# Reordering the start of an attention + expert-layer kernel: two bias-row loads, and two pairs of casts

## The chip, the core and the metric

The kernel runs on one core of a Trainium2 chip. The metric is the device time of one execution in microseconds (us). A core has five engines that each work through their own instructions in order: TensorE (PE in the profile), VectorE (DVE), ScalarE (ACT), GpSimd (POOL) and Sync (SP), which here only issues transfers. Sixteen transfer (DMA) engines move the data; transfers are issued from the queues of SP, ACT and POOL.

## The reference

Inputs are q, k, v of shape (8, 8, 576, 64), gates s of shape (8, 8, 576), w_in (512, 2048) and w_out (2048, 512), all float32. The output is (4608, 512) float32.

```python
scores = scale * np.matmul(q, k.transpose(0, 1, 3, 2))       # scale = 1/8
s_pos = np.maximum(s, 0.0)
cum = np.cumsum(s_pos, axis=-1)
bias = -(cum[:, :, :, None] - cum[:, :, None, :])
scores = np.where(causal, -1000000000.0, scores + np.minimum(bias, 0.0))
attn = softmax(scores)
x = np.matmul(attn, v)            # heads put side by side: (4608, 512)
h = x @ w_in
g = h * np.clip(h + 3.0, 0.0, 6.0) / 6.0
out = g @ w_out
```

Each of the 64 heads is one causal attention whose scores get a bias, the running sum of the gates at the key less that at the query. Then every token goes through a two-layer network with the hard-swish in between.

## The kernel before

Two heads make a pair; there are 32 pairs (NP), four to a batch. The main loop (L576) goes over the pairs. In pass p TensorE computes the transposed scores of pair p in blocks (`scores`, `corner`), the output of the attention (`av`), and the transposes of the next pair (`transpose`, L217, for pairs 0 to 8; later pairs go through a transposing DMA). From pass 4 on, groups of the first and second layer (`m1`, `m2`) stand between them. The order on every engine is the order in which the code is written: nothing is reordered by a scheduler.

What a pair needs before its scores can start:

- q and k in float32 (`load_qk`, L110, two transfers of 288 KB), in one of three buffers `raws`;
- their cast to float16 into `tok` (`cast_qk`, L188, two instructions; `tok` has two buffers);
- the transposes of `tok` on TensorE (L221, six for q and six for k) and four copies from PSUM into `qks` (L230; q's two on VectorE, k's on ScalarE or shared), one of three slots;
- the bias rows: four rows per head (partitions 64 to 67) that add the bias inside the same matmul, copied by DMA from `aug`, where they lie for all 64 heads (`load_aug`, L138, two transfers of 9 KB, one a head). The slot's lower half must have been filled by `set_stair` (L508) before.

It needs v later (`load_v`, L126 twice with 128 KB and L130 with 32 KB, in rows of 256 bytes; cast by GpSimd, `cast_v`, L200 and L201).

`aug` itself is computed at the start: VectorE takes the running sum (L545), ScalarE writes its negative as one row (L548, "the bias copy"), VectorE writes three more (L549 to L553). The first bias rows can leave only after that.

The start of the program, in the order of Sync's queue: the gates, q of pair 0, v of pair 0, q and k of pair 1; then bias rows of pair 0, which wait for `aug`; then q and k of pair 2, v of pair 1, q and k of pair 3, v of pair 2; then, from pass 0, the bias rows of pair 2, q and k of pair 4, v of pair 3; from pass 1 the bias rows of pair 3, q and k of pair 5, v of pair 4; and so on. ScalarE's queue brings k of pair 0 and constants. GpSimd issues the bias rows of pair 1, and later the weights: `next_weights` (L585) in passes 0 and 2 to 6, 1 MB for each half of w_in and 512 KB for each quarter of w_out, cast to float16 on the way. Pairs from 6 on have their bias rows issued by GpSimd as well.

Pairs are counted from 0 in this text; "pairs two and three" in the change's name are pairs 1 and 2 here.

The casts of pair 0 are on ScalarE (L559), after the bias copy. Those of all later pairs are on GpSimd; pair 1's stand behind the bias rows that GpSimd issues and behind v of pair 0. In pass p GpSimd casts q and k of pair p + 2, then v of pair p + 1 (not in pass 0), then issues weights.

Before the first data arrive, TensorE runs 44 matmuls on constants (L537).

Of the kernel before, what the change touches and what calls it, by code (L numbers as in the profile page):

```python
# [18 lines left out]
def kernel(  # L19
# [10 lines left out]
    nc = tc.nc  # L30
# [8 lines left out]
    PPB = H // 2  # L39
# [60 lines left out]
    def raw6(p):  # L100
        return raws[p % NRAW][0:96].rearrange("p (i h e d) -> p i h e d", i=2, h=2, e=6)

    def raw9(p):
        return raws[p % NRAW][:, 0 : 18 * D].rearrange("p (i t d) -> p i t d", i=2, t=9)

    def load_qk(p, i, eng):
        b, h0 = p // PPB, 2 * (p % PPB)
        src = (q, k)[i][b, h0 : h0 + 2]
        if p < NPE:
            eng.dma_start(  # L110
                out=raw6(p)[:, i].rearrange("p h e d -> p h (e d)"),
                in_=src.rearrange("h (p e) d -> p h (e d)", e=6),
            )
        else:
            eng.dma_start(
                out=raw9(p)[:, i],
                in_=src.rearrange("h s d -> (h s) d").rearrange(
                    "(t p) d -> p t d", p=128
                ),
            )  # L120

    def load_v(p, eng):
        b, h0 = p // PPB, 2 * (p % PPB)
        vraw = vraws[p % NRAW]
        for hh in range(2):
            eng.dma_start(  # L126
                out=vraw[:, hh, 0:4, :],
                in_=v[b, h0 + hh, 0:512, :].rearrange("(t p) d -> p t d", p=128),
            )
        eng.dma_start(  # L130
            out=vraw[0:64, :, 4, :],
            in_=v[b, h0 : h0 + 2, 512:SEQ, :].rearrange("h p d -> p h d"),
        )

    def load_aug(p, eng):
        for hh in range(2):
            g = 2 * p + hh
            eng.dma_start(  # L138
                out=qks[p % NQK][64:68, hh, :, 64 * hh : 64 * hh + SEQ],
                in_=aug[g : g + 1, :, :, :],  # L140
            )
# [21 lines left out]
    def next_weights(n):  # L163
        for _ in range(n):
            if w_chunks:
                fn, c = w_chunks.pop(0)
                fn(c)
# [15 lines left out]
    def cast_qk(p, eng_q, eng_k):  # L183
        tok = work.tile([128, 24 * D], F16, tag="tok", name="tok")
        if p < NPE:
            tok = tok[0:96].rearrange("p (i e h d) -> p i e h d", i=2, e=6, h=2)
            for i, eng in enumerate((eng_q, eng_k)):
                eng(out=tok[:, i].rearrange("p t h d -> p h t d"), in_=raw6(p)[:, i])  # L188
        else:
            tok = tok[:, 0 : 18 * D]  # L190
            for i, eng in enumerate((eng_q, eng_k)):
                eng(  # L192
                    out=tok[:, 9 * D * i : 9 * D * (i + 1)],
                    in_=raws[p % NRAW][:, 9 * D * i : 9 * D * (i + 1)],
                )
        toks[p] = tok

    def cast_v(p):
        vraw, va = vraws[p % NRAW], vas[p % NQK]
        nc.gpsimd.tensor_copy(out=va[:, :, 0:4, 0:64], in_=vraw[:, :, 0:4, :])  # L200
        nc.gpsimd.tensor_copy(out=va[0:64, :, 4, 0:64], in_=vraw[0:64, :, 4, :])  # L201
# [15 lines left out]
    def transpose(p, i):  # L217
        tok, qk = toks[p], qks[p % NQK]
        pt = t_bank(i == 1, "pt")
        for e in range(6):  # L220
            nc.tensor.transpose(  # L221
                pt[:, 96 * e : 96 * (e + 1)],
                tok[:, i, e].rearrange("p h d -> p (h d)"),
                ident[0:96, 0:96],
            )
        for hh in range(2):
            r = 64 * hh
            on_act = i == 1 and (hh == 0 or p % 2 == 0)
            copy = nc.scalar.copy if on_act else nc.vector.tensor_copy
            copy(  # L230
                out=qk[0:64, hh, i, r : r + SEQ].rearrange("p (t e) -> p t e", e=6),
                in_=pt[r : r + 64, 0:SEQ].rearrange("p (e t) -> p t e", e=6),
            )
# [7 lines left out]
    def crossbar_qk(p):  # L241
        J[p] = work.tile([128, 9, 128], F16, tag="jt", name="jt")
        nc.sync.dma_start_transpose(out=J[p], in_=toks[p])
# [129 lines left out]
    def norm(p, hh):  # L373
        o = O.pop((p, hh))
        if hh == 0:
            X[p] = work.tile([128, 5, 2, D], F16, tag="x", name="x")
        rl = work.tile([128, 5, 1], F32, tag="rl", name="rl")
        nc.vector.reciprocal(out=rl, in_=o[:, :, 64:65])
        nc.vector.tensor_tensor(  # L379
            out=X[p][:, :, hh, :],  # L380
            in0=o[:, :, 0:64],
            in1=rl.to_broadcast([128, 5, 64]),
            op=ALU.mult,
        )
# [121 lines left out]
    def set_stair(i, copy):  # L506
        for hh in range(2):
            copy(  # L508
                out=qks[i][64:128, hh, :, 64 * hh : 64 * hh + 640].rearrange(
                    "p i (t c) -> p i t c", c=128  # L510
                ),
                in_=stair_sb[64:128, :, None, :].to_broadcast([64, 2, 5, 128]),
            )
# [21 lines left out]
    for i in range(44):  # L535
# [9 lines left out]
    nc.vector.tensor_tensor_scan(  # L545
        out=c8, data0=ones, data1=spos, initial=0.0, op0=ALU.mult, op1=ALU.add
    )
    nc.scalar.mul(out=aug[:, 0, 0, :], in_=c8, mul=-1.0)  # L548
    nc.vector.tensor_copy(out=aug[:, 1, 1, :], in_=c8)  # L549
    r1 = work.tile([NHEADS, SEQ], F32, tag="s_all", bufs=1, name="r1")  # L550
# [5 lines left out]

    nc.vector.tensor_scalar_add(out=neg_sb, in0=masks[:, 0:128], scalar1=-65504.0)

    cast_qk(0, nc.scalar.copy, nc.scalar.copy)  # L559
    transpose(0, 0)  # L560
    load_aug(0, nc.sync)
    for p in (2, 3):
        for i in range(2):
            load_qk(p, i, nc.sync)
        if p == 2:
            load_v(1, nc.sync)
    load_v(2, nc.sync)
    transpose(0, 1)
    set_stair(2, nc.vector.tensor_copy)
    load_aug(1, nc.gpsimd)  # L570
    cast_v(0)
    cast_qk(1, nc.gpsimd.tensor_copy, nc.gpsimd.tensor_copy)
    cast_v(1)


    for p in range(NP):  # L576
        nxt = p + 1 < NP
        if p + 2 < NP:
            load_aug(p + 2, nc.sync if p < PPB else nc.gpsimd)
            cast_qk(p + 2, nc.gpsimd.tensor_copy, nc.gpsimd.tensor_copy)  # L580
            if p + 2 >= NPE:
                crossbar_qk(p + 2)
        if p and nxt:
            cast_v(p + 1)
        next_weights({0: 1, 2: 1, 3: 1, 4: 1, 5: 1, 6: 1}.get(p, 0))  # L585
        if p + 3 < NP:
            for m in (p + 3, p + 4):
                late = NPE <= m < NPE + 2
                if 3 < m < NP and late == (m == p + 3):
                    for i in range(2):  # L590
                        load_qk(m, i, nc.sync)
            load_v(p + 3, nc.sync)

        def get(i):
            if p + 1 < NPE:
                transpose(p + 1, i)
            elif nxt:
                spread(p + 1, i)

        if p < PPB:  # L600
            scores(p, 0, 0)
            scores(p, 0, 1)
            get(0)
            scores(p, 0, 2)
            corner(p)
            if p:
                av(p - 1, 1, 0)
                av(p - 1, 1, 1)
                norm(p - 1, 1)
            scores(p, 1, 0)  # L610
            get(1)
            scores(p, 1, 1)
            av(p, 0, 0)
            scores(p, 1, 2)
            if p:
                transpose_x(p - 1)
            av(p, 0, 1)
            norm(p, 0)
            continue

        if p == PPB:
            av(p - 1, 1, 0)
            av(p - 1, 1, 1)
            norm(p - 1, 1)
            scores(p, 0, 0)
            scores(p, 0, 1)
            transpose_x(p - 1)
            early[0] = False
            scores(p, 0, 2)
            get(0)  # L630
            group()
            group()
        else:
            scores(p, 0, 0)
            get(0)
            group()
            scores(p, 0, 1)
            av(p - 1, 1, 0)
            group()
            scores(p, 0, 2)  # L640
            av(p - 1, 1, 1)
            norm(p - 1, 1)
            group()
        corner(p)
        group()
        if p > NPE:
            x_done[0] = p - 1
        scores(p, 1, 0)
        get(1)
        group()  # L650
        scores(p, 1, 1)
        av(p, 0, 0)
        if p >= NPE:
            crossbar_x(p - 1)
        group()
        scores(p, 1, 2)
        if PPB < p < NPE:
            transpose_x(p - 1)
        group()
        av(p, 0, 1)  # L660
        norm(p, 0)
        group()

    p = NP - 1
# [38 lines left out]
```

## Time and profile before

Four runs took 368.99, 369.27, 369.56 and 373.45 us, a median of 369.41. The profiled execution is the one of 373.45 us; its span from the first to the last instruction is 371.6 us.

| | us busy | share of the span |
|---|---|---|
| TensorE, matmuls | 350.5 | 94% |
| VectorE | 241.3 | 65% |
| ScalarE | 223.0 | 60% |
| GpSimd | 105.8 | 28% |

The 16 transfer engines are 80 to 90% busy or more in nearly all of the first three quarters of the span, and at 10% or so in most of the last quarter. Sync's queue moves 48.26 of the 54.02 MB, GpSimd's 4.70 MB.

The page says of the chain of work that ended last: 86% of the span is TensorE's, 4% transfers, 4% VectorE's. It lists the longest idle time of TensorE ahead of the score matmuls (L292): 7.3 us that ended with the landing of bias rows, in three waits of 1.1, 3.65 and 2.5 us.

How to read what follows. Times are from the start of the span. A line of a timeline gives start, length (of all its instructions together), engine and source line, operation, output <- inputs, count, and in brackets the idle time before it and what ended it. SPq and POOLq are instruction queues that issue transfers; the time of such a line is that of issuing, not of moving the data. A line of the table by stages gives the stretch, its length, then for PE, PEld (weight loads), DVE, ACT and POOL the busy time with the number of instructions, then the granted TensorE clock, the busy share of the transfer engines and GB/s. Buffer numbers are left out of names: `qk<-aug` is any pair's bias rows, `raw` q and k in float32, `vraw` v in float32, `tok` q and k in float16.

### The profile page before, as it was taken

Reading aid. Unit: us, or ns where it says so; the run is one execution under the profiler, and the core shown is the slowest. Engines: PE = TensorE matmul, PEld = TensorE weight load, DVE = VectorE, ACT = ScalarE, POOL = GpSimd, SP = SyncE. Lnnn points to the kernel's source line nnn. Section 1 sums busy time; section 2 is a strip of 40 time slices with the busy share of each in tenths; the row PEclk is TensorE's granted clock in tenths of the full one; section 3 lists DMA queues with packets and bytes.
Section 4 is the critical chain, followed back from the end, with each engine's and each line's share of the span. In section 5 each row is a group of like instructions: output and inputs, shape, how many; then the busy total and the mean of one; then the engine's idle time right before and its main releaser. Section 6 shows DMA issues by size and latency. Waiting matters only on the chain.

```text
span 371.6 us, 7713 instructions
## 1 busy us (share of the span) xinstructions
PE 350.5 (94%) x2897; PEld 204.5 (55%) x2897; DVE 241.3 (65%) x539; ACT 223.0 (60%) x388; POOL 105.8 (28%) x201
## 2 busy tenths in 40 slices
PE   6786698979999999999999999999999999999996
PEld 6565465635555555555555555555555544444442
DVE  7474769777777877777777777777775554454531
ACT  6675687846667766666666666666666334334310
POOL 3746183443334333333333333333300000000000
PEclk9998989989999999999999999999999999999999
DMA  8999999998999999999987999998311011010012
GB/s 200 201 209 182 245 220 216 155 206 169 178 172 183 196 215 178 141 215 180 177 180 147 207 178 151 203 180 149 83 49 48 28 49 38 28 56 31 28 56 86
DMA packets 147774, 54.02 MB, mean 145 GB/s; under 512 B 137520, under 2 KB 141312, under 8 KB 147736
## 3 DMA queue, kind: packets, MB, share of 16 engines
q1 hardware_dynamic: 143736, 48.26, 66.4%
q0 software_dynamic: 3360, 4.70, 7.0%
q10 hardware_dynamic: 640, 0.56, 0.6%
q8 instruction: 23, 0.38, 0.5%
q14 instruction: 15, 0.12, 0.1%
HBM read 37.11 MB, written 9.44 MB: 125 GB/s over the span
## 4 chain that ended last, share of the span: by engine, by line
PE 86%; DVE 4%; DMA 4%; ACT 3%; POOL 1%; issue 1%; ACTq 0%
PE po L442 33%; PE ph L420 32%; PE O L356 7%; PE S L303 7%; PE S L292 4%; DMA qk<-aug 4%; ACT P L311 1%; DVE gT L431 1%; PE pt L221 1%; DVE qk L253 1%; DVE x L379 1%; ACT qk L508 1%; PE ptx L393 1%; DVE qk L230 1%; ACT tr L430 1%
## 5 line engine op out<-in xcount | busy, mean ns | idle before, releaser
L431 DVE SCALAR_TENSOR_TENSOR gT<-tr,ph 128x512 f16<-128x512 f32 x144 | 98.7, 685 | 90.5 <-ACT tr L430 89.6
L420 PE MATMUL ph<-xT,w_in_sb 128*128 128x512 f16 x576 | 149.4, 382 | 2.6 <-DVE xT L398 2.6
L430 ACT ACTIVATE tr<-ph,bias 128x512 f32<-128x512 f32 x144 | 98.9, 687 | 78.3 <-PE ph L420 68.6
L442 PE MATMUL po<-w_out_sb,gT 128*128 128x512 f16 x576 | 145.9, 379 | 0.0
L311 ACT ACTIVATE P<-S 128x512 f16<-128x512 f32 x192 | 112.3, 595 | 50.7 <-PE S L292 30.8
L420 PEld LDWEIGHTS <-w_in_sb 128*128 128x128 f16 x576 | 58.9, 113 | 39.5 <-issue 1.1
L442 PEld LDWEIGHTS <-gT 128*128 128x128 f16 x576 | 50.1, 98 | 45.7 <-issue 0.5
L138 POOL DMA_DIRECT2D qk<-aug x54 | 31.5, 584 | 130.2 <-PE Sc L325 62.1
L303 PE MATMUL S<-qk 68*128 68x448 f16 (+3 forms) x256 | 51.7, 284 | 0.5 <-ACT P L311 0.4
L356 PEld LDWEIGHTS <-P 128*128 128x128 f16 x896 | 40.9, 100 | 16.8 <-issue 3.7
L356 PE MATMUL O<-va,P 128*128 128x65 f16 x896 | 49.7, 196 | 0.2 <-ACT P L311 0.2
L303 PEld LDWEIGHTS <-qk 68*128 68x128 f16 x256 | 24.7, 102 | 23.6 <-issue 1.6
L292 PE MATMUL S<-qk 128*128 128x128 f16 (+1 forms) x256 | 26.2, 228 | 7.9 <-DMA qk<-aug 7.3
L379 DVE TENSOR_TENSOR x<-O,rl 128x320 f16<-128x320 f32 x64 | 31.5, 492 | 2.2
L253 DVE COPY qk<-jt 64x768 f16<-64x768 f16 x92 | 31.8, 346 | 1.3
L292 PEld LDWEIGHTS <-qk 128*128 128x128 f16 (+1 forms) x256 | 20.2, 102 | 22.6 <-issue 9.3
L192 POOL CAST tok<-raw 128x576 f16<-128x576 f32 x46 | 29.5, 673 | 6.4 <-DMA raw<-in_k_dram 3.5
L451 DVE TENSOR_SCALAR ob<-po 128x512 f32<-128x512 f32 x36 | 24.6, 683 | 10.1 <-PE po L442 10.1
L313 DVE TENSOR_TENSOR P<-P,masks_sb 128x512 f16<-128x512 f16 x56 | 24.7, 442 | 7.4 <-ACT P L311 7.3
L200 POOL CAST va<-vraw 128x512 f16<-128x512 f32 x32 | 19.7, 616 | 12.2 <-DMA vraw<-in_v_dram 10.2
L230 DVE COPY qk<-pt 64x576 f16<-64x576 f16 x22 | 16.6, 754 | 8.3 <-PE pt L221 6.3
L188 POOL CAST tok<-raw 96x768 f16<-96x768 f32 x16 | 12.9, 827 | 9.8 <-DMA raw<-in_q_dram 5.1
(44 smaller groups left out, 143.4 us busy)
## 6 DMA issues: line engine op xcount, KB each, us to landing
raw<-in_q_dram SPq DMA_DIRECT2D x32, 288.0 KB, 4.5
out_dram<-ob SPq DMA_DIRECT2D x36, 256.0 KB, 2.0
raw<-in_k_dram SPq DMA_DIRECT2D x31, 288.0 KB, 5.4
vraw<-in_v_dram SPq DMA_DIRECT2D x64, 128.0 KB, 4.4
w_in_sb<-in_moe_w_in_dram POOLq DMA_DIRECT2D x2, 1024.0 KB, 10.1
w_out_sb<-in_moe_w_out_dram POOLq DMA_DIRECT2D x4, 512.0 KB, 8.2
vraw<-in_v_dram SPq DMA_DIRECT2D x32, 32.0 KB, 3.7
qk<-aug POOLq DMA_DIRECT2D x54, 9.0 KB, 3.6
```

The lines of the kernel that those rows point to most:

```text
L138: eng.dma_start(out=qks[p % NQK][64:68, hh, :, 64 * hh : 64 * hh + SEQ], in_=aug[g : g + 1, :, :, :],)
L192: eng(out=tok[:, 9 * D * i : 9 * D * (i + 1)], in_=raws[p % NRAW][:, 9 * D * i : 9 * D * (i + 1)],)
L253: nc.vector.tensor_copy(out=qk[0:64, :, i, 128 * par : 128 * par + 256 * n].rearrange("p h (s two c) -> p h s two c", two=2, c=128)[:, :, ...
L292: mm(S[:, c], lhsT=kT[0:68, c] if masked else kT[:, c], rhs=qT[0:68, c] if masked else qT[:, c], start=(j == 0 and not masked), stop=(j == 3),
L303: mm(S[:, c : c + w], lhsT=kT[0:68, 128 * j : 128 * (j + 1)], rhs=qT[0:68, 128 * (j + 1) : SEQ], start=(c == 0), stop=(c != 0),)
L311: nc.scalar.activation(out=pt[:, c], in_=S, func=AF.Exp, scale=0.125)
L356: mm(o[:, i, :], lhsT=lhsT, rhs=va[:, hh, j, 0:65], **kw)
L379: nc.vector.tensor_tensor(out=X[p][:, :, hh, :], in0=o[:, :, 0:64], in1=rl.to_broadcast([128, 5, 64]), op=ALU.mult,)
L420: mm(ph, lhsT=w_in_sb[ft // 8][:, kc, c : c + 512].rearrange("p (u r) -> p r u", r=4)[:, ft % 4], rhs=xT[:, kc, n * 512 : (n + 1) * 512], ...
L430: nc.scalar.activation(out=tr, in_=ph, func=AF.Relu, bias=bias3[:, 0:1])
L431: nc.vector.scalar_tensor_tensor(out=gTs[n][:, ft, :], in0=tr, scalar=6.0, in1=ph, op0=ALU.min, op1=ALU.mult)
L442: mm(po, lhsT=gTs[n][:, ft, t4 * 128 : (t4 + 1) * 128], rhs=w_out_sb[ft // 4][:, ft % 4, :], start=(ft == 0), stop=(ft == NFT - 1),)
```

## The change

Four edits at the start of the program.

1. The casts of pair 0's q and k on ScalarE come before the bias copy instead of after it.
2. Pair 1's bias rows are issued by Sync, between q and k of pair 2 and v of pair 1, instead of by GpSimd.
3. Pair 2's bias rows are issued ahead of the loop, between v of pair 1 and q of pair 3, instead of in pass 0 behind v of pair 2. The issue stays with Sync.
4. GpSimd casts pair 1's q and k before v of pair 0, and not after it.

```diff
@@ -545,6 +545,7 @@
     nc.vector.tensor_tensor_scan(
         out=c8, data0=ones, data1=spos, initial=0.0, op0=ALU.mult, op1=ALU.add
     )
+    cast_qk(0, nc.scalar.copy, nc.scalar.copy)
     nc.scalar.mul(out=aug[:, 0, 0, :], in_=c8, mul=-1.0)
     nc.vector.tensor_copy(out=aug[:, 1, 1, :], in_=c8)
...
@@ -556,27 +557,28 @@
-    cast_qk(0, nc.scalar.copy, nc.scalar.copy)
     transpose(0, 0)
     load_aug(0, nc.sync)
-    for p in (2, 3):
-        for i in range(2):
-            load_qk(p, i, nc.sync)
-        if p == 2:
-            load_v(1, nc.sync)
-    load_v(2, nc.sync)
+    for i in range(2):
+        load_qk(2, i, nc.sync)
+    load_aug(1, nc.sync)
+    load_v(1, nc.sync)
     transpose(0, 1)
     set_stair(2, nc.vector.tensor_copy)
-    load_aug(1, nc.gpsimd)
+    load_aug(2, nc.sync)
+    for i in range(2):
+        load_qk(3, i, nc.sync)
+    load_v(2, nc.sync)
+    cast_qk(1, nc.gpsimd.tensor_copy, nc.gpsimd.tensor_copy)
     cast_v(0)
-    cast_qk(1, nc.gpsimd.tensor_copy, nc.gpsimd.tensor_copy)
     cast_v(1)
...
         if p + 2 < NP:
-            load_aug(p + 2, nc.sync if p < PPB else nc.gpsimd)
+            if p:
+                load_aug(p + 2, nc.sync if p < PPB else nc.gpsimd)
             cast_qk(p + 2, nc.gpsimd.tensor_copy, nc.gpsimd.tensor_copy)
```

## The prediction

> **What bounds the kernel now.** I read the chain of work first, because it says what the end hangs on. These are pieces of it: start, length, what.
>
> ```profile
> 9.12 0.57 POOL qk L138
> ...
> 11.70 0.78 POOL tok L188
> ...
> 12.52 0.66 PE pt L221 x6
> ...
> 22.69 7.69 DMA qk<-aug
> ...
> 40.20 5.52 DMA qk<-aug
> ```
>
> The bias rows that GpSimd issues for pair 1 delay its cast of pair 1's q, and the transpose at 12.52 waits for that cast. Both are edited. But two later pieces are ten times longer: the bias rows of pair 3 (issued 22.69) and of pair 5 (40.20), each landing over 5 us after issue. So next I looked at TensorE's timeline where they land; the bracket is the idle time before and who ended it.
>
> ```profile
> 12.52 0.66 PE L221 MATMUL pt<-ident,tok 96*128 96x96 f16 x6 [0.74 <-POOL tok L188]
> ...
> 26.48 0.38 PE L274 MATMUL S<-neg_sb,ident 128*128 128x512 f16 x1
> 30.51 0.38 PE L292 MATMUL S<-qk 68*128 68x128 f16 x4 [3.65 <-DMA qk<-aug]
> ...
> 45.85 0.37 PE L292 MATMUL S<-qk 128*128 128x128 f16 x2 [2.50 <-DMA qk<-aug]
> ```
>
> The edited wait is 0.74 us; 14 us behind it stands one of 3.65 us that a transfer ends. From about 62 us on TensorE is busy nearly throughout (234.29 of the 238 us from 62 to 300), so what arrives late at 45.85 is late at the end.
>
> Why do 9 KB take 7.7 us? Sync's timeline shows what is ahead of them on the same queue.
>
> ```profile
> 8.53 1.54 SPq L138 DMA_DIRECT2D qk<-aug  x2
> 10.11 0.43 SPq L110 DMA_DIRECT2D raw<-in_q_dram  x1
> ...
> 12.91 0.51 SPq L110 DMA_DIRECT2D raw<-in_q_dram  x1
> ...
> 15.75 1.48 SPq L138 DMA_DIRECT2D qk<-aug  x2
> ...
> 21.13 1.46 SPq L130 DMA_DIRECT2D vraw<-in_v_dram  x1
> 22.69 1.41 SPq L138 DMA_DIRECT2D qk<-aug  x2
> ```
>
> Last, busy time by stage; the last two columns are the share of the transfer engines and GB/s.
>
> ```profile
> 9.00:11.00 2.00, 0.88 (x7) 0.34 (x6) 1.93 (x4) 1.27 (x2) 1.84 (x3) 1.00 0.24 59
> 11.00:18.00 7.00, 6.26 (x56) 4.54 (x54) 2.95 (x5) 4.33 (x9) 4.46 (x8) 1.00 1.10 244
> ...
> 21.00:27.00 6.00, 5.75 (x98) 4.42 (x96) 3.71 (x8) 5.93 (x13) 2.44 (x4) 1.00 1.05 180
> ...
> 31.00:34.00 3.00, 3.00 (x42) 2.46 (x41) 2.19 (x4) 2.37 (x6) 3.00 (x6) 0.62 0.79 117
> 34.00:46.00 12.00, 8.89 (x107) 6.13 (x106) 8.86 (x18) 8.54 (x16) 3.47 (x7) 0.93 1.12 235
> ```
>
> From 11 to 31 us the transfer engines are full. The landing of pair 3's rows is thus set by how much data stands before them and by any hole in the stream, hardly by when TensorE is ready. Against 235 to 244 GB/s, the 180 from 21 to 27 stands out: there the first 1 MB of weights (issued 18.11) runs beside pair 3's v, whose packets are 256 bytes against 2048; in the packet records the two alternate, so v crawls.
>
> **The change part by part.** The profiled execution took 373.45 us (span 371.6, 1.85 around it) and is the slowest of the four runs; the median is 369.41. I work out shifts in the profiled one and add them to the median.
>
> *q0 and k0 cast before the bias copy (ACT).* The ACT stair copies end at 6.34. Two casts by the row of 1.55 us then end at 7.9, the bias copy of 0.68 at about 8.6. TensorE's first transposes move from 7.83 to about 7.2. But VectorE reads them only after L557 (ends 8.47), and pair 0's bias rows may now leave only after 8.6 instead of VectorE's end at 8.37: +0.17 us for those rows and for every load that Sync has queued behind them, and for TensorE's score matmul at 10.77, which waits for these rows. k0 landed at 6.61, before its cast can start (7.1), so no new wait there.
>
> *Pair 1's bias rows from GpSimd to Sync.* Off GpSimd: 1.58 us of issuing (9.12 to 10.69). Onto Sync: 1.54 us, the row of pair 0. Behind them in Sync's order are v1, q3, k3, v2 and everything later.
>
> *Pair 2's bias rows ahead of q3.* Their 1.48 us used to stand behind v2; now q3, k3 and v2 wait for them too. They would land some 2 us after an issue at 14.5 (pair 0's: 8.53 to about 10.6), against 19.5 now and a need at 22.7: earlier by 3 us, worth nothing.
>
> *Pair 1's q and k cast before v0 (GpSimd).* k1 landed at 10.30, so two casts (1.59) can end near 11.2 instead of 13.24; the 0.74 wait at 12.52 goes. v0 follows (1.0), done by 12.2, needed at 15.39: hidden. The next item late is v1, for which GpSimd already waits until 15.78; so the weights that it issues later stay near 18.1. The gain, 0.74 - 0.17 = 0.57 us, arrives at the wait for pair 3's rows and ends there, since TensorE only waits longer.
>
> A row speaks on GpSimd beside VectorE: one VectorE copy of f16, L253, took 2.60 us at 75.88, against a mean of 0.346, until about when GpSimd's unbroken row of work ended (78.33). The second slot's stair copies (10.10 to 11.0) now stand beside such a row, and could last to 13.1. VectorE's next copies start at 13.22 now: covered, cost 0 to 0.6 and taken as 0. The Trainium skill ("SBUF — State Buffer", "Who interferes with whom") says why: the two engines share a port pair that one holds for a whole instruction. By it alone the stair copy would wait for one cast, an estimate of 0.8 us, where the row shows several; neither reaches the path.
>
> *The price: a hole in the stream.* q3 was issued at 12.91. With 0.17, 1.54 and 1.48 before it that becomes 16.1, or 16.0 as a 0.1 us wait before it goes. An issue puts its first packet on the wire 0.9 us later (q2: 10.11, 11.0), so q3 flows from 16.9 and not, as now, right behind v1 from 14.6. v1 itself, issued from 12.75, would end near 15.2, as q2 and k2 cover its delay. So the engines have nearly nothing to do from 15.2 to 16.9, and the stream behind is up to **16.9 - 14.6 = 2.3 us** later.
>
> The Trainium skill ("DMA: Bandwidth & Descriptors", "Issuing engines are not separate DMA queues") holds the issuing time usually small beside the transfer. By that the move would be worth nothing either way; here 3.0 us of issuing stands before 0.6 MB that needs 2.5 us at 240 GB/s, so the rows decide against it.
>
> What wins some of it back: the first weights now meet more of q4 and k4 (1536-byte packets) and less of v3. From 21 to 27 the engines ran at 180 GB/s where 235 was had with q and k beside weights (34 to 46): up to 6 x (1 - 180/235) = 1.4 us. So pair 3's rows land 0.9 to 2.3 us later than 30.37. Then from 31 to 34 the engines ran at 117 GB/s, slack of 3 x (1 - 117/235) = 1.5 us, which later data can fill. At the second wait (45.85) the shift is 0.9 - 1.5, so at best none, to +2.3; I take **+1.0**, near the middle, as the hole is sure and both savings are partial. Behind it TensorE is full: +1.0 at the end, 374.4 for the profiled execution, **370.4** for the median.
>
> **Rivals.** *Slower.* v2 is the third victim. Its 256-byte packets would flow from about 19.3; if its share that is left when the weights start (20.5) is large, it crawls to about 26, as v3 does now. TensorE needs pair 2's v at 25.45 and GpSimd 0.9 us before, so this decides from a landing after 24.5. GpSimd sits in order behind it with pair 4's casts. Then all 2.3 us pass, and the longer idle time costs another window of half clock: the granted clock was 0.5 for 3.4 us after each of the two waits, 1.7 us of work. Sum +4.0: 373.4, more where pair 4's casts come late too. For it: the packet sizes and v3's crawl. Against: v2 starts 1.2 us before the weights and needs 1.4.
>
> *Faster.* The weights beside q4 and k4 run at the full 235 GB/s, the hole is smaller because the engines lag (one was 1.5 us behind at 18.1), so pair 3's rows land about 1.4 us sooner, and the waits shrink enough to keep the clock: -1.4 and one or two windows of 1.7, giving 364.6 to 366.3. For it: half clock stands after both waits. Against: it needs the hole to cost nothing.
>
> *Nothing.* The slack at 31 to 34 swallows the whole shift: 369.4, within 0.7. That the change does not do what it says I give little: no new wait holds back the GpSimd casts, but their gain of 0.57 us has nowhere to go.
>
> **The numbers.** Forecast 0.40 (0.05 of it beyond +3.7), nothing 0.13, slower rival 0.27 (0.25 beyond +3.7), faster rival 0.20 (0.18 beyond -3.7). A measurement of this kernel tells about 1%, 3.7 us, from no change. So faster 0.18, slower 0.30, the rest 0.52 within. The forecast's own range is 369.4 (all absorbed) to 371.7 (2.3 passes). To hold 8 in 10 it goes down to 366.5, near the faster rival's cheaper end, and up to 374.0, past the slower rival's 373.4: 0.1 is left out on each side.
>
> **What would show it.** Right: no idle time before pair 1's transposes; Sync issues q3 near 16; the transfer share dips in 15 to 17; the first score matmul of pair 3 starts at 31 to 32.5, though TensorE arrives near 26. Wrong: q3's packets flow without a dip; pair 3's rows land before 30; v1 or v2 lands so late that TensorE stands at attention-times-values; or the wait at 45.85 goes, which I have not foreseen.

## The result and the profile after

The changed kernel took a median of 373.34 us over 34 runs, the kernel before 370.94 over 55. The ratio is 1.006, with a 95% interval of 1.0041 to 1.0079: **slower by 2.2 us** (0.006 x 370.94). As a shift that is within the forecast's own range (0 to +2.3). The time itself, 373.34, lies above that range's 371.7, because the kernel before came out at 370.94 and not at 369.41; it is inside the range stated for 8 in 10, 366.5 to 374.0.

The two profiled executions don't show it as a sum: 373.44 us (span 371.7) after, 373.45 (span 371.6) before. The one of before has an idle time of TensorE of 2.58 us at 76.3 us, and half clock behind it, that the one of after lacks; in the other profiles of this study that gap was absent or at most 1.9 us, whatever had been edited. So I compare where pair 5's scores start, ahead of that gap (45.85 us before), and for times the medians.

The chain of waits after, in the same stretch (start, length, what):

```profile
13.00 3.68 DMA vraw<-in_v_dram
...
17.65 0.78 POOL tok L188
...
18.48 0.66 PE pt L221 x6
...
21.52 8.59 DMA qk<-aug
...
42.61 5.43 DMA qk<-aug
```

The wait for the bias rows that GpSimd issued is gone. In its place, one pair later, stands a transfer of v (pair 1), a cast of GpSimd (pair 2's q), and the transposes that need it. TensorE's timeline has the sizes:

```profile
18.48 0.66 PE L221 MATMUL pt<-ident,tok 96*128 96x96 f16 x6 [1.21 <-POOL tok L188]
...
30.25 0.38 PE L292 MATMUL S<-qk 68*128 68x128 f16 x4 [2.02 <-DMA qk<-aug]
...
48.18 0.59 PE L292 MATMUL S<-qk 128*128 128x128 f16 x4 [3.73 <-DMA qk<-aug]
```

The edited wait of 0.74 us at 12.52 is gone and one of 1.21 us has come. Pair 3's rows let TensorE go on at 30.25, where it was 30.51. But pair 5's scores start at 48.18 and not at 45.85: the whole loss of this profile, 2.33 us, lies between the two waits. GpSimd's timeline shows why:

```profile
16.81 0.61 POOL L200 CAST va<-vraw 128x512 f16<-128x512 f32 x1 [4.27 <-DMA vraw<-in_v_dram]
17.36 0.29 POOL L201 CAST va<-vraw 64x128 f16<-64x128 f32 x1
17.60 1.59 POOL L188 CAST tok<-raw 96x768 f16<-96x768 f32 x2
19.14 0.90 POOL L144 DMA_DIRECT2D w_in_sb<-in_moe_w_in_dram  x1
...
32.70 0.29 POOL L201 CAST va<-vraw 64x128 f16<-64x128 f32 x1 [1.17 <-DMA vraw<-in_v_dram]
32.94 0.77 POOL L144 DMA_DIRECT2D w_in_sb<-in_moe_w_in_dram  x1
```

Pair 1's v is cast at 16.81 (15.78 before), pair 2's q and k behind it, and the first chunk of weights leaves at 19.14 (18.11). The second chunk waits for v of pair 3 and leaves at 32.94 (31.30). Sync is held by the same landing: its issue of pair 4's rows waits for the semaphore of that last load of v.

```profile
32.71 1.38 SPq L138 DMA_DIRECT2D qk<-aug  x2
```

In seven of the eight profiles in which nothing behind the start was edited, the last share of v of pair 3 lands between 30.62 us (before) and 32.65 (changed), the second chunk leaves 0.3 to 0.7 us behind it, and pair 5's scores start 14.5 to 15.2 us behind that chunk: this is the path of the loss in them. (The eighth is the one with v of pair 1 behind q and k of pair 3.) But of the 2.03 us by which that v lands later in the changed kernel, most is one transfer engine's: the other fifteen had landed their shares by 30.34, against 30.14 before. What made that one share late was not tested (see the last section).

Busy time by stage (transfer share and GB/s are the last two columns), two stretches after:

```profile
15.00:17.00 2.00, 2.00 (x19) 1.38 (x17) 1.45 (x3) 1.19 (x3) 0.19 (x1) 0.50 0.36 60
...
33.00:35.00 2.00, 2.00 (x29) 1.78 (x27) 0.68 (x2) 1.16 (x3) 2.00 (x3) 0.74 0.45 45
```

and the same two before:

```profile
15.00:17.00 2.00, 2.00 (x22) 1.43 (x21) 0.89 (x2) 1.83 (x4) 1.22 (x3) 1.00 1.09 254
...
33.00:35.00 2.00, 2.00 (x23) 1.66 (x22) 0.65 (x2) 1.61 (x3) 2.00 (x5) 0.50 0.97 134
```

The first line of each pair shows the hole that was forecast. The second shows another one, in front of the late second chunk: the slack that I had expected to be filled had grown. The clock column (0.50 after, 1.00 before, at 15 to 17) is no difference between the kernels there: the same two score matmuls (L303, 68x320) took 0.62 us in both, at 14.98 and at 15.83, and 0.38 us at 25.69 before. The record of before has probably missed the half clock there.

### The profile page after: what moved, and what is told of

Same layout as the page of the kernel before. It is cut to its first block, busy times and chain, and to the rows that moved or that the text cites. A ratio compares the mean times of both kernels' runs of the same rounds, so it can differ in the third digit from the quotient of the medians.

```text
span 371.7 us, 7714 instructions
## 1 busy us (share of the span) xinstructions
PE 349.4 (94%) x2897; PEld 204.4 (55%) x2897; DVE 239.9 (65%) x539; ACT 223.5 (60%) x388; POOL 104.7 (28%) x199
## 4 chain that ended last, share of the span: by engine, by line
PE 83%; DMA 7%; ACT 4%; DVE 3%; SPq 1%; issue 1%; ACTq 0%; POOL 0%; POOLq 0%
PE po L442 33%; PE ph L420 31%; PE O L356 7%; PE S L303 6%; DMA qk<-aug 6%; PE S L292 3%; ACT tr L430 1%; DVE gT L431 1%; DMA vraw<-in_v_dram 1%; ACT P L311 1%; SPq L138 1%; PE pt L221 1%; ACT qk L508 1%; DVE qk L230 1%; DVE x L379 1%
## 5 line engine op out<-in xcount | busy, mean ns | idle before, releaser
L138 POOL DMA_DIRECT2D qk<-aug x52 | 29.9, 575 | 126.0 <-PE Sc L325 59.1
L303 PE MATMUL S<-qk 68*128 68x448 f16 (+3 forms) x256 | 51.6, 284 | 0.4 <-ACT P L311 0.4
L303 PEld LDWEIGHTS <-qk 68*128 68x128 f16 x256 | 24.6, 102 | 23.0 <-issue 0.8
L253 DVE COPY qk<-jt 64x768 f16<-64x768 f16 x92 | 29.8, 324 | 1.3
```

Of the source, the lines that this page charges most:

```text
L138: eng.dma_start(out=qks[p % NQK][64:68, hh, :, 64 * hh : 64 * hh + SEQ], in_=aug[g : g + 1, :, :, :],)
L253: nc.vector.tensor_copy(out=qk[0:64, :, i, 128 * par : 128 * par + 256 * n].rearrange("p h (s two c) -> p h s two c", two=2, c=128)[:, :, ...
L303: mm(S[:, c : c + w], lhsT=kT[0:68, 128 * j : 128 * (j + 1)], rhs=qT[0:68, 128 * (j + 1) : SEQ], start=(c == 0), stop=(c != 0),)
```

## The experiments

Theories when the first runs went out: **1**, the issuing time on Sync and its hole in the stream of loads cost by themselves; **2**, the late v of pair 1 costs, because GpSimd waits for it in order with pair 2's casts and the weights behind; **3**, the cast edits cost. All ratios are to the kernel before, with 95% intervals; 0.001 is 0.37 us.

**The edits apart.** Casts only (ScalarE's casts of pair 0 ahead of L548 instead of at L559):

```diff
+    cast_qk(0, nc.scalar.copy, nc.scalar.copy)
...
-    cast_qk(0, nc.scalar.copy, nc.scalar.copy)
...
+    cast_qk(1, nc.gpsimd.tensor_copy, nc.gpsimd.tensor_copy)
     cast_v(0)
-    cast_qk(1, nc.gpsimd.tensor_copy, nc.gpsimd.tensor_copy)
```

> The two cast edits alone (ScalarE's casts ahead of the bias copy, GpSimd's pair-1 casts ahead of v of pair 0); all bias rows issued where they were before. Theory 1 (issuing time on Sync delays the loads) and theory 2 (the late v of pair 1 holds GpSimd's queue) both put the loss on the moved bias rows: time of before within 0.6 us, weights issued near 18.1 us, second wait ending near 45.9 us. Theory 3 (the cast edits cost: the stair copies on VectorE took 2.68 us beside GpSimd's casts, against 0.90 before) has the loss here: about +2.2 us, ratio 1.006.

Measured 1.0043 (1.0011 to 1.0075), +1.6 us: more than theories 1 and 2 allowed, less than theory 3 asked for. Rows only (the rest of the change):

> The two moves of bias rows alone (pair 1's to Sync, pair 2's ahead of q of pair 3); casts in the old order. Theories 1 and 2: the whole loss, +1.8 to +2.6 us, the transfer share falling below 0.3 around 16 us, v of pair 1 cast near 16.8 us, weights near 19.1 us. Theory 3: within 0.6 us of before.

Measured 1.0078 (1.0044 to 1.0112), +2.9 us, so the whole loss is there without the cast edits and theory 3 falls as an account of the whole. v of pair 1 was cast at 16.66, the weights left at 19.00, and pair 5 started at 47.86. Next, the changed kernel with pair 1's rows back on GpSimd, ahead of its casts of pair 1:

```diff
-    load_aug(1, nc.sync)
...
+    load_aug(1, nc.gpsimd)
```

> The changed kernel with pair 1's bias rows back on GpSimd, ahead of its casts; pair 2's rows stay ahead of q of pair 3. v of pair 1 is then issued at about 11.2 us as before, but q of pair 3 still 1.5 us later than before. Theory 1 (only the sum of issuing time counts): about half the loss, +0.8 to +1.4 us. Theory 2 (v of pair 1 counts, because GpSimd waits for it): loss gone, within 0.6 us of before; v of pair 1 cast near 15.8 us, weights near 18.1 us.

Measured 1.0031 (1.0003 to 1.0058), +1.1 us: inside theory 1's range and above theory 2's, though the interval reaches into both. v of pair 1 was not on time here either: fifteen engines had landed it by 15.80, one at 17.20, and the weights left at 19.04. And with pair 2's rows back behind v of pair 2:

```diff
-    load_aug(2, nc.sync)
     for i in range(2):
         load_qk(3, i, nc.sync)
     load_v(2, nc.sync)
+    load_aug(2, nc.sync)
```

> The changed kernel with pair 2's bias rows back behind v of pair 2; pair 1's rows stay on Sync between k of pair 2 and v of pair 1. v of pair 1 is issued at about 12.5 us as in the changed kernel, q of pair 3 at about 14.4 instead of 15.8. Theory 1: about half the loss, +0.8 to +1.4 us. Theory 2: the whole loss, +1.8 to +2.6 us; v of pair 1 cast near 16.8 us, weights near 19.1 us.

Measured 1.0118 (1.0078 to 1.0158) in six executions, the worst: +4.4 us, beyond both ranges and nearer to theory 2's. So the parts don't add up. Between runs that differ in one edit, pair 1's rows on Sync cost in both places where they can be compared (casts only to the run with pair 2's rows late: 0.0075; the run with pair 1's rows on GpSimd to the changed kernel: 0.0029). Moving pair 2's rows forward, which makes the hole larger, cost in neither (0.0031 against 0.0043; 1.006 against 1.0118). Of these four differences only the 0.0075 has intervals that do not overlap, and those just miss each other. That speaks against the hole as such and for v of pair 1, and does not settle it. But the casts alone lost something too, which neither 1 nor 2 had expected; in that run's profile GpSimd also waited longer for v of pair 1:

```profile
17.73 0.29 POOL L201 CAST va<-vraw 64x128 f16<-64x128 f32 x1 [1.03 <-DMA vraw<-in_v_dram]
...
19.51 0.78 POOL L144 DMA_DIRECT2D w_in_sb<-in_moe_w_in_dram  x1
```

Sync had issued that v at the same time as before (11.15). One of the 16 engines landed its share at 17.68, the other fifteen by 16.27; the last section comes back to it.

**The late v, taken alone and taken away.** In the changed kernel, pair 2's casts ahead of v of pair 1 on GpSimd:

```diff
     cast_v(0)
+    cast_qk(2, nc.gpsimd.tensor_copy, nc.gpsimd.tensor_copy)
     cast_v(1)
...
-            cast_qk(p + 2, nc.gpsimd.tensor_copy, nc.gpsimd.tensor_copy)
+            if p:
+                cast_qk(p + 2, nc.gpsimd.tensor_copy, nc.gpsimd.tensor_copy)
```

> The changed kernel with one move on GpSimd: the casts of pair 2's q and k stand ahead of the cast of v of pair 1, no longer behind it. Sync's order, and so the hole in the stream of loads, stays as in the changed kernel. Theory 2 (the late v of pair 1 holds pair 2's casts and the first weights): the 1.2 us wait of TensorE at 17.3 us goes, the weights are issued near 17.8 instead of 19.1 us, and the loss goes: within 0.7 us of before. Theory 1 (the hole itself): the wait at 17.3 goes too, but the time stays +1.6 to +2.6 us.

Measured 1.0077 (1.0047 to 1.0107). The wait at 17.3 went, the weights left at 17.67, and the loss stayed: theory 2, as I had put it, fell. The profile shows where the gain was given back:

```profile
17.67 0.90 POOL L144 DMA_DIRECT2D w_in_sb<-in_moe_w_in_dram  x1
...
24.50 0.61 POOL L200 CAST va<-vraw 128x512 f16<-128x512 f32 x1 [3.30 <-DMA vraw<-in_v_dram]
26.02 0.29 POOL L201 CAST va<-vraw 64x128 f16<-64x128 f32 x1 [0.91 <-DMA vraw<-in_v_dram]
```

Now the weights start while v of pair 2, almost 3 us late behind the issued rows, is still on its way, and GpSimd waits for it to 26 us (about 22 before and after). This is the mechanism of the prediction's slower rival. This execution was the fastest of its twelve (371.37 us, a median of 373.54), and its pair 5 starts at 46.53, only 0.68 us later than before; so the profile shows a way of losing and not the whole 2.9 us. The opposite test, the kernel before with a late v of pair 1 and no issue added:

```diff
         for i in range(2):
             load_qk(p, i, nc.sync)
-        if p == 2:
-            load_v(1, nc.sync)
+    load_v(1, nc.sync)
     load_v(2, nc.sync)
```

> The kernel before, with the three loads of v of pair 1 behind q and k of pair 3 on Sync instead of ahead of them: no added issue, no hole, only a later v of pair 1 (cast near 18.3 instead of 15.8 us). Theory 2: TensorE waits for pair 2's casts near 18 us, the weights leave near 20.5 us, and the time is +2 us or more. Theory 1: no hole, no loss, within 0.7 us of before.

Measured 1.0056 (1.0023 to 1.0089): about the change's loss, with no hole (transfer share 1.03 or more from 12 to 18 us). TensorE waited 2.52 us for pair 2's casts.

```profile
20.51 0.66 PE L221 MATMUL pt<-ident,tok 96*128 96x96 f16 x6 [2.52 <-POOL tok L188]
```

A late v of pair 1 is thus enough to lose this much without a hole. But it was later here than in the change: the weights left at 21.18, 3.07 us later than before, against 1.03. And the loss took another path: pair 3's scores did not wait, and 4.18 us of waiting came at pair 4's rows (39.11). Whether 1.03 us alone loses as much was not tried.

**The long waits.** The rows of pairs 3 to 5 and v of the same pair are neighbours on Sync; this swaps them.

```diff
             load_aug(p + 2, nc.sync if p < PPB else nc.gpsimd)
+            if 1 <= p <= 3:
+                load_v(p + 2, nc.sync)
...
-            load_v(p + 3, nc.sync)
+            if p >= 3:
+                load_v(p + 3, nc.sync)
```

> The kernel before, with the bias rows of pairs 3, 4 and 5 ahead of v of the same pair on Sync (they are neighbours there; only their order changes). If what stands before the rows in Sync's queue sets the two long waits, the rows of pair 3 are issued near 19.6 instead of 22.7 us and land before 25 us, those of pair 5 near 35 instead of 40.2 us; the waits of 3.65 and 2.5 us go or shrink, and the time falls by 3 to 6 us (ratio 0.984 to 0.992). If the data as a whole set the waits (what TensorE wants next is as late), TensorE waits for v of pair 3 and for q and k of pair 6 instead, and the gain is under 1.5 us.

Measured **0.9915** (0.9886 to 0.9945), 3.1 us faster than before: the best kernel of the study, and clearly faster than both. Two lines, Sync's issue of pair 3's rows and TensorE's start on pair 3:

```profile
19.50 1.38 SPq L138 DMA_DIRECT2D qk<-aug  x2
```

```profile
27.36 0.39 PE L292 MATMUL S<-qk 68*128 68x128 f16 x4
```

There is no bracket: the first long wait is gone, and pair 5 starts at 40.20 after a wait of 0.65 us. Some of it came back as a wait for v (1.75 us at 44.3). With this swap and pair 2's casts moved, in the changed kernel:

> The changed kernel with both: pair 2's casts ahead of v of pair 1 on GpSimd, and the bias rows of pairs 3 to 5 ahead of v of the same pair on Sync. If the edits of the changed kernel are harmless once GpSimd is not held and the rows come early, it equals the run of the kernel before with rows ahead of v, within 0.8 us, or is up to 1.5 us faster since pair 1's casts come earlier. If the hole costs by itself, it is 1 to 2 us slower than that run.

Measured 1.0017 (0.9982 to 1.0051), 1.0% or 3.8 us behind the swap alone, more than either reading had allowed. TensorE's line names the place:

```profile
30.23 0.60 PE L356 MATMUL O<-va,P 128*128 128x65 f16 x8 [7.10 <-POOL va L200]
```

The weights left at 17.12, and v of pair 2, issued from 17.41, landed its last two loads only when they were through; 7.1 us of TensorE went into one wait. Again the late v pays, now by crawling and not by holding GpSimd.

**The weights out of the way.** If both ways of paying are real, the weights must be late enough not to meet v of pair 2 before the first way can be seen alone.

```diff
-        next_weights({0: 1, 2: 1, 3: 1, 4: 1, 5: 1, 6: 1}.get(p, 0))
+        next_weights({1: 1, 3: 1, 4: 1, 5: 1, 6: 1, 7: 1}.get(p, 0))
```

On the kernel before:

> The kernel before, with the chunks of weights that GpSimd issues in passes 0, 2, 3, 4, 5, 6 issued in passes 1, 3, 4, 5, 6, 7. The first chunk then leaves after the cast of v of pair 2, near 22 instead of 18.1 us, when v of pair 3 (issued 19.6 to 22.6) is mostly through. Theory 4 (what costs is a v of 256-byte packets caught beside a chunk of weights): the first wait of 3.65 us falls below 1 us, and the time falls by 2 to 5 us. Theory 5 (the amount of data before the rows costs, weights or not): the first wait shrinks too, but the second grows by as much; within 1 us of before.

Measured 0.9981 (0.9952 to 1.0009). The first wait was still 3.1 us in its profile: what comes before the rows holds them even so. Theory 4 falls; theory 5 has the time right, but the second wait, which it wanted longer, is gone in this profile, which is of the fastest execution of the twelve. On the changed kernel:

> The changed kernel with the same later chunks of weights. Theory 4: with the first chunk out of the way of every v, the change loses what it cost: within 0.8 us of the kernel before with later weights. Theory 6 (the change costs on the way to pair 1 and 2, by the late v of pair 1 that holds GpSimd and TensorE at 17.3 us, and no transfer wait hides it any more): 1.2 to 2.5 us slower than the kernel before with later weights.

Measured 1.0027 (1.0 to 1.0053), 0.0046 or 1.7 us behind its pair, where theory 4 wanted under 0.8 and theory 6 had 1.2 to 2.5. GpSimd's hold is there:

```profile
19.07 0.66 PE L221 MATMUL pt<-ident,tok 96*128 96x96 f16 x6 [1.52 <-POOL tok L188]
```

The same with pair 2's casts ahead of v of pair 1:

> The changed kernel with the later chunks of weights and with pair 2's casts ahead of the cast of v of pair 1 on GpSimd. Nothing then holds pair 2's casts, and the first chunk of weights leaves near 22 us, past v of pair 2, so neither can take the gain of the other as in the run with pair 2's casts moved alone. Theory 6 (the late v of pair 1 that holds GpSimd is what is left of the loss): the wait of TensorE near 17.5 us goes, and the time equals the kernel before with later weights, 0.995 to 1.000 of the kernel before. Theory 1 (the hole itself): the wait goes but the time stays with the changed kernel with later weights, 1.001 to 1.005.

Measured 0.998 (0.9947 to 1.0014): level in time with the kernel before with later weights, as theory 6 had it. The same transposes follow without a wait, at 17.07, the hole is still there (transfer share 0.13, 0.19 and 0.06 in the three us from 15), and pair 3's scores start at 26.72 (28.50 with the hold). But in both profiles pair 4's scores then wait for bias rows, and they start at 35.76 and 35.71: the 1.8 us gained are not seen past that wait. The intervals of the three runs touch as well, so the times fit theory 6 and do not show it. Last, the swap with later weights, for a better kernel:

> The kernel before with both: the bias rows of pairs 3 to 5 ahead of v of the same pair on Sync, and the weights one pass later. If the two remove the same wait, it is within 1 us of rows ahead of v alone (ratio 0.9915 to before); if each removes another, 1.5 to 4 us faster than that.

Measured 1.0015 (0.9982 to 1.0047): worse than the swap alone, by more than I had allowed for either way. Its profile has a wait of 2.49 us at 31.06 and one of 2.34 us at 79.13. Why the two work against each other is open.

## Why the prediction was right, and where it was not

Sign and range held: 370.4 was forecast against 369.41, +1.0, and +2.2 measured, at the upper end (+2.3) of the likeliest case. That the size came near is partly luck: of the terms that it was added up from, the hole was right, and what should have carried it to the end was not. Step by step:

- *ScalarE's casts.* The bias copy ended at 8.54 (8.6 forecast), Sync's rows left at 8.60, 0.07 us later and not 0.17. Right, and small.
- *The hole.* q3 was issued at 15.80 (16.0), its packets began at about 16.9 (16.9), the transfer share fell to 0.36 from 15 to 17. Right to 0.2 us.
- *The stair copies beside GpSimd's casts.* They took 2.68 us and ended at 12.39; the next copies began at 12.42 and nothing waited for them. Right. It agrees with the Trainium skill ("SBUF — State Buffer", "Who interferes with whom") that one engine shuts the other out; that the rule names one instruction and the copies lasted through GpSimd's whole row (9.64 to 12.5) is the measurement's addition.
- *"The weights that it issues later stay near 18.1"* is **the step that failed.** It rested on v1 ending near 15.2 as q2 and k2 "cover its delay". They didn't: v1's packets ran to 16.47, at 133 to 138 GB/s from 14.5 to 15.5, where before v1 had flowed at 215 to 221 from 14 to 15. The second of its loads, which the cast waits for, landed at 16.68 instead of 15.72; fifteen engines had their shares by 16.08, so 0.6 us of this is one engine's. GpSimd went on 1.03 us late, and a wait of 1.21 us that I had excluded came up at 17.27. The gain (0.85 us at pair 1's scores, 16.20 instead of 17.05) was used up there, and pair 2's transposes came 0.55 us later than before. None of that reached the end through TensorE, whose wait for pair 3's rows shrank by more (3.65 to 2.02 us); what was left of it was the late GpSimd.
- *Weights beside q4 and k4* hardly happened: the last of those packets ended at 22.97, half a us after the weights' first (22.47). v of pair 3 crawled as before: in each half us some 45 packets of 256 bytes against 45 of 2048. The Trainium skill ("DMA: Bandwidth & Descriptors", "Queues, rings and completion order") has each engine go round its queues, changing at packet boundaries. Equal counts agree with that, as far as the records' packets are what the page means.
- *Pair 3's rows 0.9 to 2.3 us late:* wrong; they let TensorE go at 30.25, 0.26 us earlier than before and not at 31 to 32.5, as the weights that they waited behind ended only 0.6 us later than before (the last packets start at 29.15 and 28.54).
- *The slack from 31 to 34 takes up to 1.5 us of it:* wrong in sign. It grew: from 31 to 36 us 543 KB were moved, against 745 before, since GpSimd waited for the last of pair 3's v to 32.70 and the second chunk left 1.64 us late. The +2.33 us at pair 5's start is the term that I had at +1.0.

The price was thus near and its carrier another: not the lateness of pair 3's rows behind the hole, but a v that lands late, GpSimd that waits for it in order, and the weights behind it. Two comparisons and the run with a late v and no hole speak against the hole by itself. That the added issues are what makes the v's late is shown for v of pair 1 in part (0.4 of its 0.96 us on fifteen engines) and not for v of pair 3, which Sync issued no later than before (its last load at 20.77, against 21.13). The slower rival's mechanism, v of pair 2 beside the weights, did not occur in the change itself, because the weights left later too; it appeared in two runs as soon as they left earlier.

What stays open: how much of the loss is one straggling engine, which is in the profiles of the change, of the casts alone (they cost 0.0043 without any moved transfer) and of pair 1's rows on GpSimd; whether it comes in every execution, as there is one profile of each kernel; and why pair 2's rows placed late cost more than placed early.

## What to carry to other kernels

Where a transfer of a few KB is moved onto a queue with bulk loads, ask what the loads behind it release: here 1.3 us of issuing on Sync stood before a v that came late, and that held an engine that works in order, with the casts and weights behind. A small transfer that is needed soon belongs ahead of the bulk of the same moment (swapping the rows with v gained 0.85%); what it displaces must not be what an in-order engine waits for next. And removing one wait in a start that is full of transfers pays only if no later wait on the same path takes up the gain: here the next one was 3.65 us, for a gain of 0.57.

## What was not expected of the hardware

- One transfer engine falls behind the others, by 0.6 to 2.3 us in the loads named here. Instruction packets of 16 KB on a queue of their own (q8 in the third part of the page) last 0.9 to 1.5 us each. Before, one began at 15.94, as v1 was landing (15.99); in the run with the casts alone one began at 15.52, and one engine's share of v1 came 1.4 us after the rest. In the changed kernel one began at 29.97 and lasted 1.50 us, and the last share of v of pair 3 came 2.3 us after the other fifteen. The coincidence is in the records; that it is the cause was not tried.
- A transfer issued by Sync waits on the semaphore that the transfer eight before it on Sync and ScalarE uses: before, the second load of v of pair 3 was issued at 20.33, just after that one's landing at 20.32. So a small transfer also takes one of eight places.
- A wait of TensorE can cost more than its length: its granted clock went to 0.5 after most waits of 2 us or more in these runs and after some shorter ones, mostly for 3.4 or 6.8 us, at the start of the program for up to 13.7.
